# The second layer's second product with features on the partitions; joining two attention chunks' inverses in one step

## The chip, the core and the metric

One core of a Trainium2 chip runs the whole program. The metric is the device time of one execution in microseconds (us). TensorE (PE) multiplies matrices and writes to PSUM, VectorE (DVE), ScalarE (ACT) and GpSimd (POOL) work elementwise, and SyncE (SP) issues the transfers. Each engine runs its own instructions in program order and waits on semaphores for the others.

## What is computed

Attention with a state per head (the delta rule: 4 batches, 8 heads, 768 tokens, 48 dimensions), then two dense layers over its 3072 x 384 output. Cut to what matters:

```python
for t in range(S):                       # attention, k_n is k with unit norm
    y[:, :, t] = q[:, :, t] @ state
    v_old = state.T @ k_n[:, :, t]
    state += beta[t] * outer(k_n[:, :, t], v[:, :, t] - v_old)
x = y as (3072 tokens, 384)
h = x @ w_in;   x = elu(h) @ w_out       # layer 1: 384 -> 2048 -> 384
h = x @ w_in2;  out = (h * sigmoid(1.702 * h)) @ w_out2   # layer 2
```

## The kernel before

**Attention.** The sequence is cut into 12 chunks of 64 tokens, worked on in 6 passes `p` of two chunks, `a = 2p` and `b = 2p + 1`. All 32 heads of the batch are spread over the partitions, two groups of 64 tokens, and over the free axis, 16 positions `u` of a chunk. Inside a chunk the recurrence becomes a triangular system of 64 x 64 per head, and its inverse is made from halves: `gram` (L171) multiplies keys with keys, `inverse` (L194) inverts the two 32 x 32 diagonal blocks of each head on DVE, column by column, and the chunk's steps `t2`, `m1` and `m2` (L374 to L404) make the off-diagonal block, which is minus one diagonal inverse times the off-diagonal block of `gram` times the other diagonal inverse. In tile `z` columns 0 to 31 hold the diagonal inverses and columns 32 to 63 the off-diagonal blocks. `t2` transposes the chunk's inverses on DVE; `m1` is 32 products of 32 x 32 on PE into a bank `ps_b`, two copies on ACT to `m`, a third that repeats the inverses in `z`, and two clears on POOL; `m2` is 32 more products and two more moves on ACT back to `z`. Each product in fp32 stands as two MATMULs in the trace, so `m1` and `m2` are 64 records each. In passes 0 to 2 (`FINE`) the 32 x 32 blocks are themselves joined from 16 x 16 blocks by `join16` (L297; its products are L310 and L318). Then come, chunk by chunk, `kq` (keys times queries, L357) with `mask` on DVE (L368), `ks` (keys times state, L415) and the subtraction to `r` on DVE (L420), `w` (L432), `state` (L451), `y` (L467) and `out` (L489).

Nearly all of these write one PSUM tile of two banks, `ps_w` (`wide`, one buffer): the next step that takes it waits until the last one has been read.

**Dense layers.** 512 tokens (64 tokens of two chunks for 4 batches) are a block; each layer has 6 blocks, and each block 16 units `m` of 128 hidden features. A unit is `up` (9 MATMULs of 128 x 512 into `h`, L569), an activation and a split of the result into two parts `gh` and `gl` (ACT and DVE), and, two units later (`LAG`), the second product: in the first layer `down_t` (L603), 9 MATMULs with weights stationary and 512 tokens moving into three banks `acc`, features on the partitions; in the second `down_n` (L614), 12 MATMULs with `gh` or `gl` stationary and 384 output features moving into four banks out of six, tokens on the partitions. The last unit of a block copies the sums out (`end_t`, `end_n`) and stores them.

**Order.** `schedule` (L678) writes the order by hand. The first layer's blocks run with the attention of the next pass between their units: unit `u` is `fill` (DVE steps of the next `inverse`, spread by the table `VECTOR` and the function `spread`), then the list `mid` behind `up`, then the second product of unit `u - 2`, then the list `end`. A slot `2u` in the tables means `mid` of unit `u`, a slot `2u + 1` its `end`, counted from the block's first unit. The sixth block of the first layer and the second layer have no attention beside them.

Of the kernel before, what the change touches and what calls it, by code (L numbers as in the profile page):

```python
# [9 lines left out]
F32 = mybir.dt.float32  # L10
# [10 lines left out]
P = 128  # L21
# [10 lines left out]
class Kernel:  # L32
# [90 lines left out]
    def place(self, c, name):  # L123

        if c in (0, 2):
            x, i = (self.spare[0], 0) if name == "t2" else (self.spare[1], 1024)
            return x[:, i:i + 512].rearrange("p (u t) -> p u t", u=16)
        return self.ap.tile([P, 16, 32], F32, name=name, tag=name)

# [194 lines left out]


# [234 lines left out]
    def up(self, wt, x, c0, n, act_fn):  # L560
# [3 lines left out]
        c = slice(c0, c0 + n)  # L564
        hps = self.ps_m.tile([P, TB], F32, name="h", tag="h")[:, 0:n]
        i = 0
        for k in range(NK):
            for part, src in ((0, xh), (0, xl), (1, xh)):
                nc.tensor.matmul(  # L569
                    hps, wt[:, part, k * P:(k + 1) * P], src[:, k, c], start=(i == 0), stop=(i == 3 * NK - 1)  # L570
                )
                i += 1
        t = self.mp.tile([P, TB], F32, name="t", tag="t", bufs=3)[:, 0:n]
        gh = self.mp.tile([P, TB], F32R, name="gh", tag="gh", bufs=self.LAG + 1)[:, 0:n]
        gl = self.mp.tile([P, TB], F32R, name="gl", tag="gl", bufs=self.LAG + 1)[:, 0:n]
# [22 lines left out]
    def down_t(self, wt, g, acc, m):  # L598

        gh, gl = g  # L600
        for c in range(NK):
            for i, (part, src) in enumerate(((0, gh), (0, gl), (1, gh))):
                self.nc.tensor.matmul(  # L603
                    acc[c], wt[:, part, DM + c * P:DM + (c + 1) * P], src,
                    start=(m == 0 and i == 0), stop=(m == NM - 1 and i == 2),
                )

    def down_n(self, wt, g, acc, m):

        gh, gl = g  # L610
        for w in range(NW):
            c = slice(w * P, (w + 1) * P)
            for i, (src, part) in enumerate(((gh, 0), (gh, 1), (gl, 0))):
                self.nc.tensor.matmul(  # L614
                    acc[w], src[:, c], wt[:, part, DM:2 * DM],
                    start=(m == 0 and i == 0), stop=(m == NM - 1 and i == 2),
                )

    def x1_load(self, p):
# [8 lines left out]
        def split(c):  # L628

            xh, xl = [x[:, c, :].rearrange("p (b c t) -> p b c t", b=B, c=2) for x in self.x["b", p]]  # L630
            raw = st["raw"][:, c, :].rearrange("p (c b t) -> p b c t", b=B, c=2)
# [5 lines left out]
    def end_t(self, p, c0, n, acc):  # L637

        pool, tag = (self.w2p, "xo") if p >= NP - 2 else (self.mp, "w")
        d = self.x1d[p]  # L640
        halves = [pool.tile([P, 2 * DM], F32, name="xo", tag=tag, bufs=2) for _ in range(NK * n // (2 * DM))]
        if n == TB:
            x, y, n2 = *halves, n // 2
# [392 lines left out]
```

## Time and profile before

| | us |
|---|---|
| median of 3 runs | 1036.44 (1032.35 to 1042.41) |
| the profiled execution | 1037.44 |
| its span, first to last instruction | 1035.7 |
| PE busy | 982.5 (95%) |
| DVE, ACT, POOL busy | 598.6 (58%), 453.2 (44%), 49.2 (5%) |

The profile gives each engine's busy time, the chain of work that ended last (PE holds 90% of it), and the idle time of an engine before each group of instructions with what ended it. A busy time adds durations that overlap on PE, so prices of PE work are read here from one start to the next. The mean granted clock of PE was 0.981 of full speed.

### The profile page before, as it was taken

Reading aid. Unit: us, or ns where it says so; the run is one execution under the profiler, and the core shown is the slowest. Engines: PE = TensorE matmul, PEld = TensorE weight load, DVE = VectorE, ACT = ScalarE, POOL = GpSimd, SP = SyncE. Lnnn points to the kernel's source line nnn. Section 1 sums busy time; section 2 is a strip of 40 time slices with the busy share of each in tenths; the row PEclk is TensorE's granted clock in tenths of the full one; section 3 lists DMA queues with packets and bytes.
Section 4 is the critical chain, followed back from the end, with each engine's and each line's share of the span. In section 5 each row is a group of like instructions: output and inputs, shape, how many; then the busy total and the mean of one; then the engine's idle time right before and its main releaser. Section 6 shows DMA issues by size and latency. Waiting matters only on the chain.

```text
span 1035.7 us, 26881 instructions
## 1 busy us (share of the span) xinstructions
PE 982.5 (95%) x12136; PEld 837.4 (81%) x12136; DVE 598.6 (58%) x1065; ACT 453.2 (44%) x749; POOL 49.2 (5%) x65
## 2 busy tenths in 40 slices
PE   3578898999999999999999999999999999999998
PEld 3565676877788888888888788999999999999997
DVE  5579559747887788687434777643333333333333
ACT  1254465444445445445545676533333333333332
POOL 2100000000001000000000010100000001000000
PEclk9987899999999999999999999999999999999999
DMA  5252332401220221211001921001010010100000
GB/s 193 103 176 101 113 111 96 134 34 54 72 82 30 79 72 53 74 52 52 33 2 62 371 117 61 1 1 61 1 62 1 1 61 1 41 22 1 31 1 31
DMA packets 20179, 68.41 MB, mean 66 GB/s; under 512 B 3168, under 2 KB 6240, under 8 KB 20064
## 3 DMA queue, kind: packets, MB, share of 16 engines
q1 hardware_dynamic: 20064, 66.69, 18.5%
q8 instruction: 95, 1.56, 0.6%
q14 instruction: 20, 0.16, 0.1%
HBM read 57.25 MB, written 9.44 MB: 64 GB/s over the span
## 4 chain that ended last, share of the span: by engine, by line
PE 90%; DVE 5%; issue 2%; DMA 1%; ACT 1%; SPq 0%; ACTq 0%
PE h L569 39%; PE acc L603 19%; PE acc L614 10%; PE accn L614 10%; PE ps_w L467 2%; PE ps_w L357 1%; PE ps_w L183 1%; PE ps_b L399 1%; PE ps_b L384 1%; PE ps_w L415 1%; PE ps_w L432 1%; PE ps_w L451 1%; PE ps_w L489 1%; PE ps_b L310 1%; PE ps_b L318 1%
## 5 line engine op out<-in xcount | busy, mean ns | idle before, releaser
L569 PE MATMUL h<-xh,wt 128*128 128x512 f32 x1152 | 401.6, 403 | 7.3 <-DVE wt L548 5.1
L569 PEld LDWEIGHTS h<-xh,wt 128*128 128x128 f32 x1152 | 219.3, 191 | 55.0 <-DVE wt L548 7.0
L569 PE MATMUL h<-xl,wt 128*128 128x512 f32 x576 | 229.5, 398 | 0.0
L603 PE MATMUL acc<-gh,wt 128*128 128x512 f32 x576 | 198.8, 399 | 0.5 <-DVE xo L667 0.5
L591 ACT CAST gh<-t 128x512 fp32r<-128x512 f32 x192 | 119.4, 622 | 177.1 <-DVE t L582 121.0
L594 DVE TENSOR_TENSOR gl<-t,gh 128x512 fp32r<-128x512 f32 x192 | 138.4, 721 | 68.7 <-PE acc L614 31.0
L588 DVE TENSOR_TENSOR t<-t,h 128x512 f32<-128x512 f32 x96 | 66.0, 688 | 180.2 <-ACT t L585 180.1
L585 ACT ACTIVATE t<-h 128x512 f32<-128x512 f32 x96 | 57.4, 598 | 198.8 <-PE h L569 198.7
L603 PEld LDWEIGHTS acc<-gh,wt 128*128 128x128 f32 x576 | 109.7, 190 | 25.2 <-issue 1.2
L569 PEld LDWEIGHTS h<-xl,wt 128*128 128x128 f32 x576 | 110.0, 191 | 19.4 <-DVE xl L495 0.2
L603 PE MATMUL acc<-gl,wt 128*128 128x512 f32 x288 | 113.8, 395 | 0.0
L582 DVE SCALAR_TENSOR_TENSOR t<-t,h 128x512 f32<-128x512 f32 x96 | 65.7, 684 | 76.2 <-ACT t L579 75.6
L578 ACT ACTIVATE t<-h 128x512 f32<-128x512 f32 x96 | 57.4, 598 | 99.3 <-PE h L569 98.5
L614 PE MATMUL acc<-wt,gh 128*128 128x384 f32 x384 | 98.4, 337 | 0.0
L614 PE MATMUL accn<-wt,gh 128*128 128x384 f32 x384 | 98.0, 336 | 0.0
L614 PEld LDWEIGHTS accn<-wt,gh 128*128 128x128 f32 x384 | 70.9, 188 | 5.5
L614 PEld LDWEIGHTS acc<-wt,gh 128*128 128x128 f32 x384 | 70.3, 188 | 2.8
L614 PE MATMUL acc<-wt,gl 128*128 128x384 f32 x192 | 64.8, 338 | 0.0
L614 PE MATMUL accn<-wt,gl 128*128 128x384 f32 x192 | 64.7, 337 | 0.0
L603 PEld LDWEIGHTS acc<-gl,wt 128*128 128x128 f32 x288 | 55.0, 191 | 10.6
L579 ACT ACTIVATE t<-t 128x512 f32<-128x512 f32 x96 | 60.7, 632 | 3.1
L633 POOL TENSOR_TENSOR xl<-x1r,xh 128x512 fp32r<-128x512 f32 x18 | 24.1, 1339 | 412.7 <-ACT xh L632 322.1
(143 smaller groups left out, 940.0 us busy)
## 6 DMA issues: line engine op xcount, KB each, us to landing
raw<-in_w SPq DMA_DIRECT2D x32, 768.0 KB, 6.7
kt<-in_kT SPq DMA_DIRECT2D x12, 512.0 KB, 4.1
x<-in_qT SPq DMA_DIRECT2D x24, 256.0 KB, 4.1
kg<-in_kT SPq DMA_DIRECT2D x10, 512.0 KB, 4.5
vn<-in_vn SPq DMA_DIRECT2D x12, 384.0 KB, 4.0
kn<-in_kn SPq DMA_DIRECT2D x12, 384.0 KB, 3.3
x1d<-xo SPq DMA_DIRECT2D x12, 384.0 KB, 2.9
x1r<-x1d SPq DMA_DIRECT2D x6, 768.0 KB, 4.5
```

The source lines that it names most:

```text
L467: pe.matmul(ps[hf][self.tok(ab), hs(u)], g["x"][k][:, 8 * hf + u, :], su[k][:, hf, hs(u)], start=True, stop=True,)
L569: nc.tensor.matmul(hps, wt[:, part, k * P:(k + 1) * P], src[:, k, c], start=(i == 0), stop=(i == 3 * NK - 1))
L578: nc.scalar.activation(out=t, in_=hps, func=AF.Relu, scale=-1.0)
L579: nc.scalar.activation(out=t, in_=t, func=AF.Exp, scale=-1.0)
L582: nc.vector.scalar_tensor_tensor(out=t, in0=t, scalar=-1.0, in1=hps, op0=ALU.add, op1=ALU.max)
L585: nc.scalar.activation(out=t, in_=hps, func=AF.Sigmoid, scale=1.702)
L588: nc.vector.tensor_tensor(out=t, in0=t, in1=hps, op=ALU.mult)
L591: nc.scalar.copy(gh, t)
L594: nc.vector.tensor_tensor(out=gl, in0=t, in1=gh.bitcast(F32), op=ALU.subtract)
L603: self.nc.tensor.matmul(acc[c], wt[:, part, DM + c * P:DM + (c + 1) * P], src, start=(m == 0 and i == 0), stop=(m == NM - 1 and i == 2),)
L614: self.nc.tensor.matmul(acc[w], src[:, c], wt[:, part, DM:2 * DM], start=(m == 0 and i == 0), stop=(m == NM - 1 and i == 2),)
L633: nc.gpsimd.tensor_tensor(out=xl, in0=raw, in1=xh.bitcast(F32), op=ALU.subtract)
```

## The change

1. **Second layer.** `down_n` goes; both layers use one `down` with weights stationary, 512 tokens moving and three accumulators (`ps_n` banks for even blocks, `ps_m` banks for odd). The output leaves as (block, feature, token), in tiles of 512 and 256 columns, and the host brings it back to tokens by features. Tokens stay in the order of the first layer, so the split of its output into `xh` and `xl` reads straight through.
2. **Off-diagonal blocks.** For passes 1 to 5 a new `across` does `t2`, `m1` and `m2` once for both chunks. Even `u` multiply from the left first, as before; odd `u` from the right, with the transposed inverse, which puts their results in the other partitions of the same bank. `m1` so fills all 128 partitions of one bank (one copy on ACT), and `m2` writes the two banks of `ps_w` (two moves on ACT of 32 x 1024).
3. **Order.** `ks` of pass 3 to 5 moves from slot 9 to 8, `m1` from 6 to 7; other slots, and three entries of `VECTOR`, as in the diff.

```diff
-        if c in (0, 2):
+        if c == 0:
...
+    def places(self, p):
+        if p == 1:
+            t, m = self.spare[0][:, 0:1024], self.spare[1][:, 1024:1536]
+            return t.rearrange("p (u t) -> p u t", u=32), m.rearrange("p (u t) -> p u t", u=16)
+        t = self.ap.tile([P, 16, 64], F32, name="kg", tag="kg").rearrange("p u (b t) -> p (u b) t", b=2)
+        return t, self.ap.tile([P, 16, 32], F32, name="m1", tag="m1")
...
+    def across(self, p):
+        nc, pe, act = self.nc, self.nc.tensor, self.nc.scalar
+        s, own = self.pas[p], {}
+        def t2():
+            own["t2"], own["m1"] = self.places(p)
+            nc.vector.transpose(out=own["t2"], in_=s["z"][:, :, 0:32])
+        def m1():
+            z, t = s["z"], own["t2"]
+            ps = self.bank().rearrange("p (v t) -> p v t", v=16)
+            for u in range(32):
+                for o in (0, 64):
+                    near, far = slice(o, o + 32), slice(o + 32, o + 64)
+                    if u % 2:
+                        pe.matmul(ps[far, u // 2, :], z[near, u, 32:64], t[near, u, :], start=True, stop=True)
+                    else:
+                        pe.matmul(ps[near, u // 2, :], z[far, u, 32:64], z[far, u, 0:32], start=True, stop=True)
+            act.copy(own["m1"], ps)
+            act.copy(z[:, :, 32:64], z[:, :, 0:32])
+            for o in (0, 64):
+                nc.gpsimd.memset(z[o + 32:o + 64, :, 0:32], 0.0)
+        def m2():
+            z, t, m = s["z"], own["t2"], own["m1"]
+            ps = self.wide().rearrange("p b (v t) -> p b v t", v=16)
+            for u in range(32):
+                for o in (0, 64):
+                    near, far = slice(o, o + 32), slice(o + 32, o + 64)
+                    a, b = (m[far, u // 2, :], z[far, u, 32:64]) if u % 2 else (t[near, u, :], m[near, u // 2, :])
+                    pe.matmul(ps[near, u % 2, u // 2, :], a, b, start=True, stop=True)
+            for o in (0, 64):
+                near = slice(o, o + 32)
+                act.activation(
+                    out=z[near, :, 32:64].rearrange("p (v b) t -> p b v t", b=2), in_=ps[near], func=AF.Copy, scale=-1.0
+                )
...
-    def down_t(self, wt, g, acc, m):
-
+    def down(self, layer, p, m, g):
+        if m == 0:
+            self.acc = self.sums(layer, p)
         gh, gl = g
+        wt = self.wt[layer, m]
         for c in range(NK):
             for i, (part, src) in enumerate(((0, gh), (0, gl), (1, gh))):
...
-    def down_n(self, wt, g, acc, m):
...
+    def sums(self, layer, p):
+        if layer and p % 2 == 0:
+            return [self.ps_n.tile([P, TB], F32, name=f"accn{c}", tag=f"accn{c}", bufs=1) for c in range(NK)]
+        return [self.ps_m.tile([P, TB], F32, name=f"acc{c}", tag=f"acc{c}", bufs=1) for c in range(NK)]
...
+        for p in range(1, NP):
+            for name, f in zip(("t2", "m1", "m2"), self.later(lambda p=p: list(self.across(p).values()), 3)):
+                ch[2 * p][name] = f
+                del ch[2 * p + 1][name]
...
-            (4, 2, "kq"), (4, 2, "mask"), (7, 2, "nv"), (9, 2, "t2"), (9, 2, "m1"), (10, 3, "kq"), (10, 3, "mask"),
-            (11, 2, "m2"), (12, 3, "t2"), (12, 3, "m1"), (13, 2, "ks"), (14, 3, "m2"), (15, 2, "w"), (17, 2, "state"), (17, 3, "nv"),
+            (4, 2, "kq"), (4, 2, "mask"), (7, 2, "nv"), (10, 2, "t2"), (10, 3, "kq"), (10, 3, "mask"),
+            (11, 2, "m1"), (12, 2, "ks"), (13, 2, "m2"), (15, 2, "w"), (17, 2, "state"), (17, 3, "nv"),
...
-                (6, a, "t2"), (6, a, "m1"), (8, a, "m2"), (10, a, "kq"), (11, a, "ks"), (12, b, "t2"), (12, b, "m1"), (13, a, "w"), (14, b, "m2"),
+                (8, a, "kq"), (9, a, "t2"), (10, a, "m1"), (11, a, "ks"), (12, a, "m2"), (14, a, "w"),
             ) if p in self.FINE else (
-                (6, a, "t2"), (6, a, "m1"), (6, a, "kq"), (8, a, "m2"), (9, b, "t2"), (9, b, "m1"), (9, a, "ks"), (11, b, "m2"), (11, a, "w"),
+                (6, a, "t2"), (6, a, "kq"), (7, a, "m1"), (8, a, "ks"), (9, a, "m2"), (11, a, "w"),
             )
```

The order on PE in a unit of the second layer, before: the end of `up` and the second product (`accn` and `acc` are its accumulators, the bracket names what a row waits for).

```order
L569 MATMUL h<-xl,wt 128x512
L569 MATMUL h<-xh,wt 128x512
L614 MATMUL accn_8446<-wt,gh 128x384 [waits Activation_49]
L614 MATMUL accn_8446<-wt,gh 128x384
L614 MATMUL accn_8446<-wt,gl 128x384 [waits DVE_49]
L614 MATMUL accn_8447<-wt,gh 128x384 x2
L614 MATMUL accn_8447<-wt,gl 128x384
L614 MATMUL accn_8448<-wt,gh 128x384 x2
L614 MATMUL accn_8448<-wt,gl 128x384
L614 MATMUL acc_8449<-wt,gh 128x384 x2
```

And now:

```order
L616 MATMUL h<-xl,wt 128x512
L616 MATMUL h<-xh,wt 128x512
L653 MATMUL accn_9296<-gh,wt 128x512 [waits Activation_49]
L653 MATMUL accn_9296<-gl,wt 128x512 [waits DVE_49]
L653 MATMUL accn_9296<-gh,wt 128x512
L653 MATMUL accn_9297<-gh,wt 128x512
L653 MATMUL accn_9297<-gl,wt 128x512
L653 MATMUL accn_9297<-gh,wt 128x512
L653 MATMUL accn_9298<-gh,wt 128x512
L653 MATMUL accn_9298<-gl,wt 128x512
L653 MATMUL accn_9298<-gh,wt 128x512
L616 MATMUL h<-xh,wt 128x512 [waits DVE_49]
```

Twelve MATMULs of 384 columns have become nine of 512, and one weight tile's two parts now stand still instead of `gh` and `gl`.

The order on PE in the second pass, where `gram` of the third pass (L183, from `kg`) takes `ps_w`. Before, it stands behind `ks` of chunk 2 (L415):

```order
L415 MATMUL ps_w<-su_88,kt 64x48 x2
L415 MATMUL ps_w<-su_92,kt 64x48 x2
L415 MATMUL ps_w<-su_88,kt 64x48
L183 MATMUL ps_w<-kg 32x64 [waits DMAHW1_49,DVE_49]
L183 MATMUL ps_w<-kg 32x64 x63
L569 MATMUL h<-xh,wt 128x512
```

Now it stands behind the joined `m2` (L365 of the changed kernel; `gram` is L191 there, and `xl` and `xh` are spare tiles that hold `m1` and `t2`):

```order
L365 MATMUL ps_w<-xl,xh 32x32 x2
L365 MATMUL ps_w<-z,xl 32x32 x2
L191 MATMUL ps_w<-kg 32x64 [waits DMAHW1_49,PE_49,Activation_49]
L191 MATMUL ps_w<-kg 32x64 x63
L616 MATMUL h<-xh,wt 128x512
L616 MATMUL h<-xl,wt 128x512
```

`gram` waited for DVE, which reads `ks` out of `ps_w`; now it waits for ACT, which reads `m2` out of it.

The order on DVE in the fifth pass around `r`, behind the first `t2`, the mask and the first steps of the next pass's `inverse`; before (L594 is `gl` of unit 3, L582 the activation of unit 4, L375 `t2` of chunk b, L420 the subtraction to `r`, the others steps of `inverse`):

```order
L240 SCALAR_TENSOR_TENSOR na<-na,dg 128x32
L241 SCALAR_TENSOR_TENSOR nb<-nb,na 128x32
L594 TENSOR_TENSOR gl<-t,gh 128x512
L582 SCALAR_TENSOR_TENSOR t<-t,h 128x512
L375 STREAM_TRANSPOSE t_4805<-z 128x512
L420 TENSOR_TENSOR r<-vn,ps_w 128x768
L239 RECIPROCAL na<-nb 128x32
```

And now (L641 is `gl`, L468 the subtraction to `r`, L629 the activation):

```order
L248 SCALAR_TENSOR_TENSOR na<-na,dg 128x32
L249 SCALAR_TENSOR_TENSOR nb<-nb,na 128x32
L641 TENSOR_TENSOR gl<-t,gh 128x512
L468 TENSOR_TENSOR r<-vn,ps_w 128x768
L629 SCALAR_TENSOR_TENSOR t<-t,h 128x512
L247 RECIPROCAL na<-nb 128x32
L248 SCALAR_TENSOR_TENSOR na<-na,dg 128x32
```

The second transposition is gone from here (the first, ahead of the mask, now has 128 x 1024), and `r` stands ahead of unit 4's activation.

## Rows read from the trace of the kernel before

**Rows 1.** Busy time by stage: stretch, length, each engine's busy time (instructions), granted clock, DMA.
```profile
300.00:571.00 271.00, 270.47 (x4067) 220.93 (x4066) 182.66 (x361) 134.82 (x221) 8.77 (x14) 1.00 0.16 52
...
627.00:1027.74 400.74, 400.74 (x2008) 362.59 (x2007) 161.13 (x227) 141.19 (x235) 19.41 (x15) 1.00 0.06 22
```

**Rows 2.** Chain that ended last, second layer: start us, us, what.
```profile
642.90 2.08 PE h L569 x9
...
1018.12 1.58 PE acc L614 x9
1019.70 2.08 PE h L569 x9
```

**Rows 3.** Timeline of PE, first layer without attention: start us, us, engine, line, operation.
```profile
581.36 0.39 PE L569 MATMUL h<-xh,wt 128*128 128x512 f32 x1
...
583.40 0.39 PE L603 MATMUL acc<-gh,wt 128*128 128x512 f32 x1
...
622.16 0.39 PE L569 MATMUL h<-xh,wt 128*128 128x512 f32 x1
```

**Rows 4.** Timeline of PE, attention's third pass (idle time before and its releaser in brackets).
```profile
211.79 1.26 PE L310 MATMUL ps_b<-kg,z 32*32 32x16 f32 x128
...
215.25 1.38 PE L318 MATMUL ps_b<-w 16*32 16x16 f32 x128
...
237.75 1.15 PE L415 MATMUL ps_w<-su,kt 48*64 48x48 f32 x64 [0.74 <-DVE x L368]
...
244.48 1.15 PE L432 MATMUL ps_w<-r,z 64*64 64x48 f32 x64
...
247.83 1.20 PE L399 MATMUL ps_b<-m,t 32*32 32x32 f32 x64
...
251.22 0.94 PE L451 MATMUL ps_w<-su,kn 64*48 64x48 f32 x64
```

**Rows 5.** Timeline of PE, attention blocks of the fourth and fifth pass.
```profile
349.04 1.15 PE L415 MATMUL ps_w<-su,kt 48*64 48x48 f32 x64
...
354.43 1.15 PE L432 MATMUL ps_w<-r,z 64*64 64x48 f32 x64
...
375.14 2.07 PE L467 MATMUL ps_w<-su,x 128*64 128x48 f32 x64
...
403.80 1.20 PE L384 MATMUL ps_b<-z 32*32 32x32 f32 x64
...
410.37 1.20 PE L399 MATMUL ps_b<-m,t 32*32 32x32 f32 x64
...
413.76 1.20 PE L384 MATMUL ps_b<-z 32*32 32x32 f32 x64
...
420.28 1.20 PE L399 MATMUL ps_b<-m,t 32*32 32x32 f32 x64
...
426.79 0.94 PE L451 MATMUL ps_w<-su,kn 64*48 64x48 f32 x64
```

**Rows 6.** Timeline of DVE beside the first of those blocks, fifth pass.
```profile
405.14 0.72 DVE L375 STREAM_TRANSPOSE t<-z 128x512 f32<-128x512 f32 x1
406.16 2.80 DVE L368 TENSOR_TENSOR x<-ps_w,mask_p 64x512 f32<-64x512 f32 x4 [0.30 <-PE ps_w L357]
...
412.79 0.68 DVE L582 SCALAR_TENSOR_TENSOR t<-t,h 128x512 f32<-128x512 f32 x1
413.38 0.70 DVE L375 STREAM_TRANSPOSE t<-z 128x512 f32<-128x512 f32 x1
416.11 0.96 DVE L420 TENSOR_TENSOR r<-vn,ps_w 128x768 f32<-128x768 f32 x1 [2.02 <-PE ps_w L415]
```

**Rows 7.** Timeline of PE, then of ACT: the product of `gram` behind `ks`, second pass.
```profile
139.73 1.47 PE L183 MATMUL ps_w<-kg 48*32 48x64 f32 x127 [1.08 <-DVE r L420]
...
141.25 1.01 ACT L189 COPY z<-ps_w 128x1024 f32<-128x1024 f32 x1 [2.83 <-PE ps_w L183]
```

**Rows 8.** Busy time and granted clock in two stretches of the second pass.
```profile
123.40:133.70 10.30, 9.82 (x89) 7.63 (x90) 6.97 (x10) 2.77 (x5) 0.00 (x0) 0.50 0.07 17
```

## Prediction before the run

> **What bounds the kernel now.** First the busy time by stage: from 300 us on PE is busy all the time (270.47 of 271.00 us beside the last passes of attention, 400.74 of 400.74 in the second layer) at a granted clock of 1.00, while DVE has 182.66 and 161.13 [rows 1]. So past 300 us time is the sum of what PE does, and every microsecond that PE saves is a microsecond of the kernel, unless a saving makes PE wait. The reader should then leave busy times aside, since records on PE overlap, and measure from start to start. Two such clocks tick in the trace. In the second layer a unit's `up` starts at 642.90 and, 90 units later, at 1019.70 [rows 2]: 376.80 / 90 = 4.187 us for 9 MATMULs of 512 columns and 12 of 384. In the first layer, where no attention is left, `up` starts at 581.36 and ten units later at 622.16 [rows 3]: 4.080 us for 18 MATMULs of 512 columns, and `up` alone takes 583.40 - 581.36 = 2.04.
>
> Attention's blocks stand between these products. With 2.04 for half a unit, a block's price is the distance to the next block less 2.04 for each half between. In the third pass `m2` of one chunk (64 records) costs 251.22 - 247.83 - 2.04 = 1.35, `w` 247.83 - 244.48 - 2.04 = 1.31, and the 128 records of `join16` 215.25 - 211.79 - 2.04 = 1.42 [rows 4]. That 128 small products cost hardly more than 64 is the point on which the second part rests.
>
> **Second layer.** Both layouts stream the same columns (12 x 384 = 9 x 512 = 4608), so nothing is gained by columns. But the changed unit has exactly the shapes of the first layer's unit, stationary weights of 128 x 128 and 512 columns moving, and that one's time is in the trace. I take it: 4.187 - 4.080 = 0.107 less for each of 94 units, and for the last two second products, which have no `up` beside them, (4.187 - 2.08) - 2.04 = 0.067 each: 94 x 0.107 + 2 x 0.067 = **10.2 us**. The trace does not show these shapes with the second layer's activation beside them; it shows them with the first layer's, which has DVE and ACT busier, and PE did not wait there. The evacuations and stores keep their number and bytes and lie beside PE; at the very end four moves and four stores remain as before, which I cost at nothing (half a microsecond either way).
>
> The Trainium skill has a rule that speaks against this gain: "TensorE: Matmul & The Clock Gate", section "Back-to-back issue gap", gives a MATMUL of N columns N/2.4 + 2.5 ns. By it, as an estimate, 12 steps of 384 take 1950 ns and 9 of 512 take 1942 ns, and the layer would gain 0.7 us, not 10.2. The measured steps do not follow it: 2.04 us for nine is 227 ns each [rows 3], and 4.187 - 2.08 for twelve is 176 ns each [rows 2].
>
> **Off-diagonal blocks, PE.** The number of small products stays: `m1` and `m2` of two chunks, 64 records each, become two blocks of 128. What changes is that a block now goes round four places of the array (rows and columns of 32) where it went round two. No row shows these blocks. From below they are bounded by the fastest row of 128 records, `join16`'s L310, 1.26 us, which also goes round four places [rows 4]. From above by twice the present record, 2 x 1.20, plus the 0.15 that a block costs beyond its records (1.35 - 1.20): 2.55. I take 1.42, by the row of the same tile height and the same four places. One objection is that in `m2` even and odd `u` share columns of the array. Two rows answer it: `y` (L467), whose two places share all rows and not the columns, takes 2.07 us, and `ks` (L415), with as many records and the same weight width, whose four places share columns pairwise, takes 1.15 [rows 5]. Sharing columns did not cost it.
>
> Passes 3, 4 and 5. Before: `m1` with `kq` 410.37 - 403.80 - 4.08 = 2.49; `m2` 413.76 - 410.37 - 2.04 = 1.35; `m1` with `ks` 420.28 - 413.76 - 4.08 = 2.44; `m2` with `w` 426.79 - 420.28 - 4.08 = 2.43; together 8.71 [rows 5]. Now five blocks stand alone: `kq`, `ks` and `w` at 1.31 (`ks` alone: 354.43 - 349.04 - 4.08 [rows 5]; `w` above; `kq` taken as `ks`), `m1` and `m2` at 1.42: 6.77. Saved 1.94 a pass.
>
> What this makes late: `m2` now writes `ps_w`, so it waits until DVE has read `ks` out of it, and behind `m2` on PE stands everything. In the fifth pass DVE was free for `r` at 416.11 - 2.02 = 414.09. The second transposition (0.71) and unit 4's activation (0.59) no longer stand ahead, and the first transposition is twice as long (0.72 more, of which DVE's idle 0.30 takes a part): 414.09 - 0.71 - 0.59 + 0.42 = 413.21, and `r` takes 0.96 [rows 6], so `ps_w` is free at 414.17. PE would be there at 403.80 + 1.31 + 2.04 + 1.42 + 2.04 + 1.31 + 2.04 = 413.96. So a new wait of 0.2 to 0.3; I take 0.3, for passes 3 and 4. In pass 5 no `inverse` is beside it and nothing waits. If the transposition of 128 x 1024 took half as much again (0.7 more), the waits would be 0.7 longer each. Sum: 2 x (1.94 - 0.3) + 1.94 = **5.2 us**.
>
> Pass 2. Before, four blocks at 1.35; now two at 1.42: 2.56 saved. `kq` moves a unit ahead, so the 0.74 that `ks` waited for the mask [rows 4] should go. Against that, `m1` now needs `t2` (odd `u`): 1.44 of transposition, plus 1 us that I allow for the join's last subtraction and copy ahead of it, less the `up` of 2.04 in between: 0.35, between 0 and 1. 2.56 + 0.74 - 0.35 = **2.95 us**.
>
> Pass 1. Again 2.56. But `gram` of the third pass stands right behind `m2`, in the same `ps_w`. It waited 1.08 us for DVE's `r`; now it waits for two moves of 32 x 1024 on ACT, and a move of 1024 columns takes 1.01 [rows 7]: at least 2.0, and up to 3 if ACT comes to them late. I take 2.5, 1.4 more than before: **1.15 us**. The cover that hides ACT's moves elsewhere, two products between `m2` and `w`, is missing only here.
>
> ACT and POOL have fewer and longer instructions (three copies and two moves for ten), which frees ACT; I cost it at nothing, since past 300 us no engine but PE sets the end.
>
> **Sum.** 10.2 + 5.2 + 2.95 + 1.15 = 19.5 us off the profiled execution's 1037.44: 1017.9. The median of the runs is 1.0 below the profiled execution, so the prediction is **1017 us**.
>
> **The rivals.**
> - *The blocks do not overlap.* If four places go no faster than two, a block costs 2.55, not 1.42. For `m2` alone that is 5 x 1.13 = 5.7 and 1023; for both 11.3 and 1028. For it: no row has these places. Against it: L310 and L415 as above.
> - *The 384-column step is not what costs.* If the second layer's 0.107 came from what lies beside PE there and not from the shape, the new unit would take 4.187 again: 1017 + 10.2 = 1027. Against it: between 642.90 and 1019.70 most units have one activation beside them and DVE has 161.13 us in 400.74 [rows 1, 2], against a denser first layer that is faster. By the rule of the Trainium skill named above ("TensorE: Matmul & The Clock Gate"), the layer's gain would be 0.7 and the time some 1026.5.
> - *The clock falls.* In the second pass, from 123.40 to 133.70, the granted clock was 0.50, that is 1.2 GHz instead of 2.4, while DVE and ACT were mostly idle [rows 8]. It fell in a stretch of small products with waits between, and the change lies just there, with a longer wait of `gram`. One more such stretch costs 10.3 x 0.5 = 5.2: 1022; two, 1027. One fewer gives 1012.
> - *The other side: each turn drains the array.* If alternating between two directions made every small product run alone, as in `y`, where 64 records take 2.07 [rows 5], a block would take 4.14 + 0.15 = 4.3, 2.9 more, and ten blocks 29 us: 1046, slower than before. It decides from 1.42 + 19.5 / 10 = 3.4 us a block. Against it: L310 and L415 change place with every product. "TensorEngine Tiling (Array Packing)", section "Key Properties", of the Trainium skill says that a change of tiling mode drains TensorE; the blocks keep one tile size, and no run here shows a mode change by itself.
>
> **How the numbers follow.** The sum as it stands 0.62 (its own range 1012 to 1022); no overlap 0.12 (`m2` alone 0.07, both 0.05); the step 0.05; the clock worse 0.15; the drain 0.03; better than the sum by a clock stretch fewer and no new waits 0.03. A measurement of this kernel can tell about 1%: faster is below 1026, slower above 1047. Faster: 0.62 + 0.07 + 0.12 (of the clock) + 0.03 + 0.01 = 0.85. Same: 0.05 + 0.04 + 0.03 + 0.01 = 0.13. Slower: 0.02 of the drain. The range 1009 to 1027 takes in the sum, the better case, `m2` alone, and nearly all of the clock: some 0.86, with the drain and both blocks left out.
>
> **What would show it.** Second layer: `up` to `up` 4.08 us to the end. Blocks: `m1` and `m2` with 128 records in about 1.25 us, one each a pass; 2.4 would be the first rival, 4 the last. Waits: `m2` for DVE's `r` in passes 3 and 4 by some tenths, `gram` behind `m2` for ACT by 2 to 3 us near 135 us, none in pass 5. Clock: 0.50 in no more stretches than before. The prediction is wrong if the second layer keeps 4.19, if a block is over 2 us, or if PE waits more than 3 us in all past 200 us.

## The result and the profile after

The changed kernel took 1020.54 us (median of 4 runs, 1015.85 to 1026.91) beside 1035.67 us of the kernel before (median of 4 runs on the same chip): a ratio of 0.985, 95% interval 0.981 to 0.989. That is 15 us of a predicted 19.5, inside the range of 1009 to 1027. Three further series of the same two kernels, below, gave 0.986, 0.981 and 0.984. The runs of the changed kernel lie further apart than those of the kernel before (20 runs: 1013.8 to 1029.4, standard deviation 4.3; 50 runs: 1031.3 to 1042.6, 2.6), and most of this study is about why.

The profiled execution was one of the short ones, 1015.85 us, 21.6 less than the profiled one of before. Busy time by stage, as in [rows 1] (stretch, length, each engine's busy time and instructions, granted clock, DMA share, GB/s):

```profile
300.00:558.00 258.00, 257.55 (x3915) 209.09 (x3914) 176.39 (x344) 124.07 (x198) 8.21 (x8) 1.00 0.17 53
611.00:1005.00 394.00, 394.00 (x1740) 326.25 (x1739) 163.99 (x231) 143.21 (x238) 19.78 (x15) 1.00 0.07 23
```

PE is as full as it was, at a granted clock of 1.00, so whatever it saved past 300 us is in the time. The second layer in the chain that ended last (start us, us, what), as in [rows 2]:

```profile
985.76 2.04 PE h L616 x9
...
1002.08 2.04 PE h L616 x9
```

Four units from `up` to `up` take 16.32 us, 4.08 each, where [rows 2] had 4.187: the first layer's pace to the hundredth. The same chain in the last pass of attention, where [rows 4, 5] had four blocks for the pair of chunks:

```profile
486.57 1.08 PE ps_w L463 x64
487.65 2.27 PE acc L653 x9
489.92 1.22 PE ps_w L365 x82
491.13 2.26 PE h L616 x9
493.40 2.04 PE acc L653 x9
495.44 1.08 PE ps_w L480 x64
```

L463 is `ks`, L365 the new `m2` (of its 128 records the chain counts 82, since they overlap), L480 `w`. From `ks` to `w` are 8.87 us with three half units of 2.04 between: 2.75 for `ks` and `m2` together. `m2` takes 1.22 for its 128 records, the 1.2 that 64 took before [rows 5].

In the second pass (pass 1, as passes are counted from 0), `gram` behind `m2` (timeline of PE, idle time before and its releaser in brackets), and the DVE rows in the fifth pass on which a term rested, `t2` (L341), the mask (L416) and `r` (L468):

```profile
134.82 2.19 PE L191 MATMUL ps_w<-kg 48*32 48x64 f32 x128 [2.14 <-ACT z L368]
```

```profile
396.65 1.24 DVE L341 STREAM_TRANSPOSE kg<-z 128x1024 f32<-128x1024 f32 x1
397.82 2.76 DVE L416 TENSOR_TENSOR x<-ps_w,mask_p 64x512 f32<-64x512 f32 x4
...
403.56 0.95 DVE L468 TENSOR_TENSOR r<-vn,ps_w 128x768 f32<-128x768 f32 x1
```

`gram` waited for ACT's two moves, 2.14 us, as foreseen (2.5). `r` did not come late: it began at 403.56, 0.06 after `ks` had ended, and was through 1.2 us before `m2` began at 405.69. So the new wait of `m2` that I had put at 0.3 in two passes isn't there.

### The profile page after: what moved, and what is told of

The parts are those of the page before. It is cut to its first block, busy times and chain, and to the rows that moved or that the text cites. A ratio compares the mean times of both kernels' runs of the same rounds, so it can differ in the third digit from the quotient of the medians.

```text
span 1014.1 us, 26233 instructions
## 1 busy us (share of the span) xinstructions
PE 961.2 (95%) x11848; PEld 787.4 (78%) x11848; DVE 598.5 (59%) x1060; ACT 441.0 (43%) x719; POOL 48.6 (5%) x55
## 4 chain that ended last, share of the span: by engine, by line
PE 91%; DVE 4%; issue 2%; DMA 2%; ACT 1%; SPq 0%; ACTq 0%; DVEq 0%
PE h L616 39%; PE acc L653 29%; PE accn L653 10%; PE ps_w L515 2%; PE ps_w L191 1%; PE ps_w L405 1%; PE ps_w L463 1%; PE ps_w L480 1%; PE ps_w L499 1%; PE ps_w L537 1%; PE ps_b L326 1%; PE ps_b L318 1%; DMA raw<-in_w 1%; DMA kg<-in_kT 1%; DVE wt L596 1%
## 5 line engine op out<-in xcount | busy, mean ns | idle before, releaser
L653 PE MATMUL acc<-gh,wt 128*128 128x512 f32 x864 | 293.4, 394 | 0.5 <-DVE xo L714 0.5
L653 PEld LDWEIGHTS acc<-gh,wt 128*128 128x128 f32 x864 | 163.1, 189 | 35.8 <-issue 0.9
L641 DVE TENSOR_TENSOR gl<-t,gh 128x512 fp32r<-128x512 f32 x192 | 138.7, 722 | 70.6 <-ACT gh L638 70.4
L653 PE MATMUL acc<-gl,wt 128*128 128x512 f32 x432 | 169.1, 391 | 0.0
L629 DVE SCALAR_TENSOR_TENSOR t<-t,h 128x512 f32<-128x512 f32 x96 | 65.7, 684 | 75.5 <-ACT t L626 74.9
L653 PE MATMUL accn<-gh,wt 128*128 128x512 f32 x288 | 96.4, 389 | 0.0
L653 PEld LDWEIGHTS acc<-gl,wt 128*128 128x128 f32 x432 | 81.7, 189 | 16.5 <-DVE gl L641 0.3
L653 PEld LDWEIGHTS accn<-gh,wt 128*128 128x128 f32 x288 | 54.1, 188 | 11.2
L653 PE MATMUL accn<-gl,wt 128*128 128x512 f32 x144 | 56.0, 389 | 0.0
L585 DVE SCALAR_TENSOR_TENSOR w<-raw,w 128x768 uint32<-128x768 uint32 x32 | 33.7, 1053 | 0.9
L416 DVE TENSOR_TENSOR x<-ps_w,mask_p 64x512 f32<-64x512 f32 x44 | 30.2, 685 | 5.6 <-PE ps_w L405 5.1
L191 PE MATMUL ps_w<-kg 48*32 48x64 f32 x1280 | 17.2, 251 | 16.6 <-DMA kg<-in_kT 12.6
```

Source lines behind the costliest of these rows:

```text
L191: self.nc.tensor.matmul(o[q:q + 32], k[:, 32 * sub:32 * sub + 32], x, start=True, stop=True)
L416: v.tensor_tensor(out=g["x"][k][self.tok(k), 8 * hf:8 * hf + 8], in0=i, in1=self.mask_p[t].unsqueeze(1).to_broadcast(list(i.shape)), op=AL ...
L585: v.scalar_tensor_tensor(out=bits[m], in0=words(m, 0), scalar=29, in1=bits[m], op0=ALU.logical_shift_right, op1=ALU.bitwise_or)
L629: nc.vector.scalar_tensor_tensor(out=t, in0=t, scalar=-1.0, in1=hps, op0=ALU.add, op1=ALU.max)
L641: nc.vector.tensor_tensor(out=gl, in0=t, in1=gh.bitcast(F32), op=ALU.subtract)
L653: self.nc.tensor.matmul(self.acc[c], wt[:, part, DM + c * P:DM + (c + 1) * P], src, start=(m == 0 and i == 0), stop=(m == NM - 1 and i == 2),)
```

## The experiments

Each profiled execution can be cut at two points that all kernels have: the first `state` of pass 1 (chunk 2) and that of pass 5 (chunk 10, the last pass), both rows of 64 products on PE. The kernel before and the changed one, in the timelines of PE:

```profile
152.19 0.94 PE L451 MATMUL ps_w<-su,kn 64*48 64x48 f32 x64
...
512.66 0.94 PE L451 MATMUL ps_w<-su,kn 64*48 64x48 f32 x64
```

```profile
148.64 0.94 PE L499 MATMUL ps_w<-su,kn 64*48 64x48 f32 x64
...
500.75 0.94 PE L499 MATMUL ps_w<-su,kn 64*48 64x48 f32 x64
```

The table has all profiles of this study cut so, in us. "Stands" counts the places in passes 2 to 5 where PE stopped for over a microsecond inside `m2`.

| kernel | execution | to `state` of pass 1 | passes 2 to 5 | rest of the span | stands in `m2` |
|---|---|---|---|---|---|
| before | 1037.44 | 152.2 | 360.5 | 523.1 | 0 |
| l2_only | 1029.39 | 153.8 | 360.6 | 513.3 | 0 |
| across_only | 1036.60 | 154.3 | 357.6 | 523.0 | 1 |
| changed | 1015.85 | 148.6 | 352.1 | 513.4 | 0 |
| after_third | 1016.55 | 150.0 | 351.4 | 513.4 | 0 |
| after_fourth | 1025.02 | 148.8 | 361.2 | 513.3 | 2 |
| after_again | 1029.39 | 153.1 | 361.2 | 513.3 | 2 |
| two_places | 1022.60 | 149.4 | 358.2 | 513.3 | 0 |
| v_late | 1021.80 | 149.4 | 357.3 | 513.4 | 1 |
| v_late_gram | 1017.95 | 147.2 | 355.7 | 513.4 | 1 |
| m2_split | 1020.92 | 152.2 | 353.6 | 513.4 | 0 |
| m2_split3 | 1021.61 | 152.8 | 353.6 | 513.5 | 0 |
| halves2 | 1033.49 | 152.0 | 353.1 | 526.7 | 0 |

**The two halves of the change, each alone.** One kernel has the diff's second layer only (`up`, `down`, `sums`, `end_x1`, `end_out` and the layout of `out`), the other its blocks only (`places`, `across`, the slots, `VECTOR`).

> Only the second layer's change: down products of 512 columns with the weights held still; the off-diagonal blocks as in the kernel before. My sum gives 10.2 us off the kernel before (a unit of layer 2 goes from 4.19 to 4.08 us, the stretch before layer 2 stays where it was). The rival that the 384-column step is not what costs gives at most 0.7 us. If the change gained by something that needs both halves, this one and across_only together give clearly less or more than the whole.

> Only the off-diagonal blocks of both chunks at once, with their new places in the order; layer 2 as before. My sum gives 9.3 us off the kernel before (passes 3 to 5: 5.2, pass 2: 2.95, pass 1: 1.15); the trace of the changed kernel read stage by stage says 12 (passes 3 to 5: 5.1, pass 2: 4.0, pass 1: 4.0, less 0.8 for a stretch of half clock). Layer 2 keeps 4.19 us a unit.

Beside 1037.29 us of before, l2_only took 1028.57 (4 runs; ratio 0.991, 0.987 to 0.995) and across_only 1032.94 (10 runs: nine between 1022.24 and 1037.08, and one of 1043.42 that the ratio leaves out; 0.995, 0.992 to 0.999). The second layer's gain is in the right place and has the right size: the table's last part is 9.8 us shorter in l2_only and 0.1 in across_only. The blocks alone gave 4.4 us in the median where 9.3 were expected, with a spread of 15 us among the nine. The waits of PE past 200 us in the profile of across_only (what, released by, total us, times, longest) begin with a line that the kernel before does not have (its longest "issue" there is 0.8, in `join16`):

```profile
PE ps_w L365 <- issue: 2.7, 1, 2.7
```

**The changed kernel again.** Nothing edited; the second of these series stands beside the v load's experiment, the third beside the split.

> The changed kernel unaltered, to see how far its own runs lie apart: its first four were 1015.85, 1016.23, 1024.86 and 1026.91 us. If the 10 us between the pairs belong to the chip or to the run, the new ones fall at about 1016 and at about 1025 again, and the profile of a long one has the ten microseconds in one place (a load at the start, a fetch, a stretch of half clock). If they were an accident of that one session, all lie within 3 us of each other.

> The changed kernel unaltered once more, as the measure for the others of this call: 1016 to 1029 us by its eight runs so far, about 1020 in the middle. In its long profile (1029.39 us) the second product of the blocks stood 2.8 us with nothing to wait for in the third and the sixth pass, while a 16 KB block of PE's instructions came in only behind the packets of a v load; in its short profile (1015.85 us) it did not. If that is what parts long runs from short ones, a profile of this run shows such stands when it is long and none when it is short.

> The changed kernel unaltered, as the measure for the split beside it: 1014 to 1029 us by its fourteen runs so far (mean 1020.5). Its profile has a stand of 2 to 3 us in a second product if a 16 KB block of PE's instructions begins to come in over a microsecond late there, and none if it does not.

1020.83 us (4 runs), 1018.06 (6) and 1021.01 (6), beside 1037.29, 1039.73 and 1036.45 of before. Two of the profiles fell on long executions and one more on a short one, and the table parts them: with no stand passes 2 to 5 take 351.4 and 352.1, with two 361.2. Nine microseconds lie there, and the whole gain of the blocks with them, since before had 360.5. The last pass of after_fourth, to be read against the chain of the changed kernel above:

```profile
494.75 1.12 PE ps_w L365 x76
495.86 2.54 issue
498.40 0.31 PE ps_w L365 x11
498.71 3.13 PE h L616 x9
501.84 2.80 PE acc L653 x9
504.64 1.08 PE ps_w L480 x64
```

PE stops for 2.54 us near the end of `m2` and waits for nothing that the profile shows ("issue"). The two half units behind it take 3.13 and 2.80 instead of 2.26 and 2.04. Busy time and granted clock of the stand, and of the stretch behind it:

```profile
495.86:498.40 2.54, 0.00 (x1) 0.00 (x0) 0.00 (x0) 0.00 (x0) 0.00 (x0) 1.00 0.03 8
499.90:503.30 3.40, 3.40 (x9) 2.64 (x8) 0.13 (x1) 2.12 (x3) 0.00 (x0) 0.50 0.02 5
```

After the stand the granted clock was 0.50 (1.2 GHz of 2.4) for 3.40 us, though PE had work without a gap. So this stand cost 2.5 us and some 1.7 more behind it (half of 3.40). Of the seven stands that the table counts, five are followed by such a stretch. The other stand of after_fourth has 2.62 and 1.7 more, which makes 8.6 of the nine microseconds.

What PE lacks there are instructions, as the rest of this section shows. `m2` is 128 MATMULs and as many weight loads, 256 instructions in 1.3 us; elsewhere a whole unit of 4.08 us has 36. PE's instructions come in by DMA queue q8 in blocks of 16 KB: 93 blocks for the 23788 instructions of the changed kernel, 99 for the 25520 of halves2, so some 256 to a block. Traffic by queue (packets, MB, share) from the start of `ks` to the start of `m2`, first in the short execution of the changed kernel, then in after_fourth, and last in after_fourth from the start of `m2` to the end of the stand:

```profile
q1 hardware_dynamic: 16, 0.05, 8.8%
q8 instruction: 1, 0.02, 2.4%
```

```profile
q1 hardware_dynamic: 20, 0.06, 7.5%
```

```profile
q1 hardware_dynamic: 124, 0.33, 25.2%
q8 instruction: 1, 0.02, 1.6%
```

In the short execution the block comes in before `m2` begins (at 488.00, `m2` at 489.85), in after_fourth while `m2` runs (496.08, `m2` at 494.68). That holds for every profile in which `m2` is whole: without a stand in passes 2 and 5 the block began at least 1.2 us ahead of `m2`, with one it began between 0.2 us ahead of it and 1.6 behind.

The count of instructions says the same. Number PE's instructions in order of time from the start of the trace (weight loads, MATMULs and PE's own waits): the seven stands come after 10177 of them (pass 2) or 18369 (pass 5), both 193 more than a multiple of 256. In the thirteen profiles of the table PE stands 124 times for over half a microsecond before 560 us without a semaphore to wait for. Every one of the 124 comes after such a number of instructions, and each time PE goes on 1.2 to 1.6 us after a block has come in. So the stands are borders between blocks of instructions. They are not new: the kernel before has eight of them before its first `state` of pass 1, 12.7 us in all, and one in `join16`, beside the row that the prediction took for its price:

```profile
224.07 0.46 PE L310 MATMUL ps_b<-kg,z 32*32 32x16 f32 x34 [0.83 <-issue]
```

What the change did is to put `m2` there. At these two borders the 256 instructions up to the border lasted 6.5 and 6.2 us in the kernel before; in the short execution of the changed kernel they last 3.4.

The Trainium skill ("Runtime: NRT & Kernel Launch", section "Instruction fetch mechanics") has an engine's instructions refilled in blocks of 16 KiB, 256 instructions, and calls a block's border mostly hidden. The blocks agree; hidden it is at these places in the kernel before, and not in the changed one when a block comes late.

**Is it the load in front of the block?** In both long profiles the v load of the second chunk (q1 above, 384 KB) came in just then. In v_late it is held back until ACT is through with `m2`'s copies; v_late_gram moves chunk 5's `gram` away from behind `m2` too.

```diff
+        if gate:
+            self.nc.scalar.copy(t[:, 0, 0:1], self.one)
...
-        at(end, 7, lambda: self.load_v(3))
+        at(end, 7, lambda: self.load_v(3, gate=True))
...
-            at(end, o + 5, lambda b=b: self.load_v(b))
+            at(end, o + (6 if late else 5), lambda b=b: self.load_v(b, gate=True))
...
-                self.passes(at, spread, end, fill, p, (3, 6), (9, o + 2), lambda: turned(2))
+                self.passes(at, spread, end, fill, p, (3, 5), (9, o + 2), lambda: turned(2))   # v_late_gram only
```

> The changed kernel with the v load of the second chunk of passes 1 to 5 held back until ScalarE is through with the copies of the second product (a one-column copy into its tile ahead of it, and in pass 2 one unit later), so that it no longer runs while that product's 256 instructions are fetched. Theory (the load in front of the fetch is what stalls the product): no stand of 2 to 3 us in the second product, all runs between 1013 and 1021, median about 1016, some 4 us under the changed kernel's of this call. Rival (the runs part by the half-clock stretches alone, 37 to 44 us of them per run): the median and the spread stay as they are, within 1 us and 3 us.

> The same with the Gram product of chunk 5 half a unit earlier, beside the first product of pass 1 and not behind the second, where it waits 2.14 us for ScalarE's copies. If that wait is what I missed of pass 1's gain, the product waits under 0.5 us there and the state of chunk 2 comes 1.5 to 2.1 us earlier than in v_late; total about 1014. If the clock or another engine sets the end of that stretch, the wait goes and the state comes less than 0.7 us earlier.

v_late took 1021.25 us (6 runs, 1015.23 to 1027.55), no less than the changed kernel beside it (1018.06), and its last pass has a stand of 1.71 us. In that stretch no data moved at all. Chain, then traffic from 492 to 498 us:

```profile
492.35 1.12 PE ps_w L367 x76
493.47 1.71 issue
495.17 0.31 PE ps_w L367 x11
495.48 3.78 PE h L618 x9
```

```profile
q8 instruction: 1, 0.02, 1.4%
```

The block came late (492.22, `m2` at 492.28) with its road empty, so a block can be late without the load, and the load as the one cause fell. It may still make a late block later. In the five stands with the load beside, the block began 1.4 to 1.6 us behind the start of `m2`, among the load's last packets, and PE stood 2.54 to 2.83 us; in the two without, of v_late and v_late_gram, it began 0.1 and 0.2 us ahead, and PE stood 1.71 and 1.38. v_late_gram (1018.77, 5 runs, 1017.95 to 1022.89, where 1014 were expected) lost the wait of 2.14 for ACT and got another in its place: `gram` now stands right behind `m1`, 512 instructions in a row, and the chain of the second pass shows 1.47 us of "issue" before its second half, and 1.22 inside `m2`. Its `state` of pass 1 came 2.2 us earlier than in v_late, about what was expected if the wait for ACT was what that pass lacked, but less than the same stretch varies between executions of one kernel.

```profile
126.75 1.47 issue
128.22 1.04 PE ps_w L193 x61
...
134.91 0.92 PE ps_w L367 x64
135.83 1.22 issue
```

**What the four places bring.** The same products, even heads first, then odd ones, in both blocks:

```diff
-            for u in range(32):
+            for u in (*range(0, 32, 2), *range(1, 32, 2)):
```

> The changed kernel with the same products of the blocks in another order: all even heads first, then all odd ones, so that two places of the array take turns at a time and not four. My theory (four places in turn are what makes a block of 128 records cost 1.3 us) expects a block of 2.4 us, ten blocks so, 1.1 us each: 9 to 11 us more than the changed kernel, and passes 3 to 5 longer by 2.2 each. The rival (the saving came from making one block of two, with fewer copies and changes between blocks, and not from the places) expects blocks of 1.3 us and no change beyond 1 us.

1022.51 us (4 runs, 1022.02 to 1024.03). The last pass:

```profile
492.54 1.08 PE ps_w L463 x64
...
495.89 2.05 PE ps_w L365 x126
...
502.24 1.08 PE ps_w L480 x64
```

`m2` takes 2.05 us with two places in turn and 1.22 with four; from `ks` to `w` 9.70 for 8.87. So a block costs 0.83 more, and passes 2 to 5, with eight blocks, take 6 to 7 us more than in the executions of the changed kernel without stands. The places are the cause, at a smaller price than the 1.1 a block that I had named. No stand fell in `m2` here, but the profile cannot say whether a slower block rides out a late block of instructions, since none was late: in passes 2 and 5 they began 1.8 and 1.7 us ahead of `m2`. Four runs within 2 us of each other hint at it, but they are four.

**Cutting `m2`.** Half of it, 128 instructions, at its slot and half one slot later, in passes 2 to 5; the copies behind the second half (m2_split) or behind each half (m2_split2). m2_split3 is m2_split2 with `m2` of pass 1 cut too, and chunk 5's `gram` behind `w`.

```diff
-                (8, a, "kq"), (9, a, "t2"), (10, a, "m1"), (11, a, "ks"), (12, a, "m2"), (14, a, "w"),
+                (8, a, "kq"), (9, a, "t2"), (10, a, "m1"), (11, a, "ks"), (12, a, "m2"), (13, a, "m2b"), (14, a, "w"),
...
-                (6, a, "t2"), (6, a, "kq"), (7, a, "m1"), (8, a, "ks"), (9, a, "m2"), (11, a, "w"),
+                (6, a, "t2"), (6, a, "kq"), (7, a, "m1"), (8, a, "ks"), (9, a, "m2"), (10, a, "m2b"), (11, a, "w"),
```

> The changed kernel with the second product of passes 2 to 5 cut in two halves of 64 products, half a unit apart, with the copies behind the second half. A half takes 128 instructions at once and not 256. Theory (a block of 256 instructions that comes late by 2 to 3 us stands the array only where the whole next block is eaten in 1.3 us): no stand in the second product in any pass, the passes 2 to 5 as in the changed kernel without stands (96, 84.5, 87.5, 84.3 us from state to state), all runs under 1021, median 2 to 4 us below the changed kernel's. Rival (stands fall where they will, or the half-clock stretches alone part the runs): median within 1 us of the changed kernel's and runs up to 1027 still. If w, one slot behind the second half, has to wait for the copies, 0.5 us or more show there in each pass.

> The split of the second product in passes 2 to 5 again, now with ScalarE's copies behind each half, so that only half of them stand between the second half and w. In the split's profile w waited 0.4 us for them in passes 3, 4 and 5. If that is so, these waits go (1.3 us in all), no second product of passes 2 to 5 stands, and the runs lie between 1015 and 1021, median about 1018. If the stands in second products were chance and not tied to 256 instructions at once, some run goes above 1024 as in every series of the changed kernel so far, and the profile of it has a stand there.

> The same, with the second product of pass 1 cut too and the Gram product of chunk 5 one unit later, behind w, instead of right behind the second product. There it waited 2.1 us for ScalarE in nearly every profile, and stood 1 to 2.5 us more in four of six with nothing to wait for. If these are what kept pass 1 from its gain, the stretch from the first up product to the state of chunk 2 falls from 69.7 to 76.7 us (changed kernel, four profiles) to 68 to 73, and the total to 1014 to 1017. If the half-clock stretches there set its length, it stays in 70 to 77 and the total with m2_split2.

1018.91 us for m2_split (5 runs, 1017.19 to 1022.10), beside 1021.01 of the changed kernel; 1019.91 for m2_split3 (6 runs, 1014.95 to 1023.07); five runs of m2_split2 lie between 1019.92 and 1027.26, and its profiled execution, at 5247.93, gives no rows. Runs over 1024 were the sign that I had named for stands by chance, and two of the five are clearly over it; no profile tells what they stood for. Passes 2 to 5 took 353.6 in the two profiles, with no stand over a microsecond inside a half. The price of m2_split is the wait that I had named, `w` for the copies, 0.4 us in three passes (the chain calls it "issue", but ACT's second copy ends just then, at 500.37):

```profile
494.19 0.68 PE ps_w L367 x50
...
497.13 0.68 PE ps_w L367 x50
...
500.08 0.38 issue
500.47 1.15 PE ps_w L484 x64
```

In passes 2 and 5 of the two profiles the block began in time, 1.7 us ahead of `m2`, at all places but one, and these say nothing of the cut. The one late block is in pass 2 of m2_split3: it began at 241.38, 1.5 us behind the start of `m2` (239.89). There the second half reads:

```profile
242.91 0.48 PE ps_w L367 x38
243.40 0.20 issue
243.59 0.39 PE ps_w L367 x24
```

From its first product to its last, `m2` took 4.09 us there for 3.71 elsewhere, so a block as late as those behind the stands of 2.5 to 2.8 us cost 0.4.

But the 16 runs of the three together have a mean of 1020.9, the 20 of the changed kernel 1020.5. So no better kernel came of it. In m2_split3 pass 1 from the first `up` to `state` took 70.5 us, inside what was expected, but the first `up` itself came at 82.3 instead of 75.5, and nothing was left of it.

**What a product costs beside its columns.**

```diff
+                for n in (slice(0, 256), slice(256, 512)) if layer else (slice(0, 512),):
...
-                    self.acc[c], wt[:, part, DM + c * P:DM + (c + 1) * P], src,
...
+                        self.acc[c][:, n], wt[:, part, DM + c * P:DM + (c + 1) * P], src[:, n],
```

> The changed kernel with each down product of layer 2 cut into two of 256 columns, with the same weights each time: 18 products a unit for 9. By the rows of before and after, a product costs its columns over 2.4 GHz and some 14 ns more (384 columns 176 ns, 512 columns 227 ns): 18 x (106.7 + 14) = 2.17 us a unit for 2.04, 12 us more in all. With 2.5 ns a product (the other reading of the same saving) it is 0.02 us a unit and 2 us in all. If a weight load of 128 columns does not fit under 256 columns of product, more than 12.

1033.49 us in one run, 13 more than the changed kernel's mean; the last part of the table grew by 13.3, where 12 were expected. The chain:

```profile
802.06 2.15 PE accn L655 x18
804.22 2.07 PE h L616 x9
806.28 2.15 PE accn L655 x18
```

A unit takes 4.22 for 4.08, 0.14 more for nine more products and not one column more: some 15 ns a product. The steps are now 227 ns for 512 columns, 176 for 384 and 2.15 / 18 = 119 for 256: each the columns at 2.4 GHz and some 13 to 16 ns more. The 2.5 ns of "TensorE: Matmul & The Clock Gate" (section "Back-to-back issue gap" of the Trainium skill) do not hold for these products with a weight load each; that section itself gives them for a product alone, and says that in a stream of weight loads and products both set the spacing. Not all of the gain is in these steps. Of the 0.107 a unit, 0.067 lies in the second product (4.187 - 2.08 = 2.107 before, 2.04 now) and 0.04 in `up`, which took 2.08 beside products of 384 columns, takes 2.07 beside those of 256 and 2.04 beside its own shape; no run isolates why.

## Why the prediction was right, and where it was not

- **Second layer, 10.2 us: right.** The rest of the span past pass 5 is 9.6 to 9.8 us shorter in every kernel that has it (the end of the kernel after PE's last product, which I had costed at nothing, takes 0.4 more: PE's part alone is 10.1), 4.08 us a unit, and halves2 shows that a product costs some 15 ns beside its columns. That is the cause of 0.067 of the 0.107 a unit; the 0.04 in `up` came in with the row of the whole unit, and its cause stays open. The rival that the 384-column step does not cost anything fell.
- **Blocks, 1.42 each: right.** From `m1` to the next block and from `m2` to `w` are 1.44 beyond the half units, in passes 3 and 5; two_places shows 2.27 without the rotation. The rival "blocks do not overlap" fell, and that each turn drains the array, too.
- **Passes 3 to 5, 5.2 us: right in the sum, with two errors in it.** In the changed kernel's profile they save 1.68, 1.69 and 1.72. I had 1.94, less 0.3 for `r` in two of them. The wait for `r` does not exist; against it `m1` and `m2` cost 1.44 and not 1.42, and `m1` 0.25 more in pass 4, a stand that ends at 399.9, at a border of instruction blocks (after 15553 instructions, again 193 more than a multiple of 256). Some 0.2 in passes 3 and 5 is left without a cause.
- **Pass 2, 2.95 us:** 3.3 in the same profile (99.0 to 95.8 us from `state` to `state`). By its own terms `m1`'s wait for `t2` is 1.44 + 1 - 2.04 = 0.40, not 0.35; that changes nothing here.
- **Pass 1, 1.15 us: borne out only as an estimate.** `gram`'s wait was 2.14 for a foreseen 2.5. But the stretch up to `state` varies from 148.6 to 154.3 in six profiles with the changed order, mean 151.1, and had 152.2 and 153.8 in the two with the old. The 3.6 us that the first pair of profiles shows must not be read as the change's gain; 1.9 is the difference of the means, with a spread larger than itself. Stands of over half a microsecond at instruction borders go with it. In the six they come to 9.0, 11.7, 12.4, 13.7, 14.6 and 14.9 us up to `state`, for 148.6, 148.8, 150.0, 152.0, 153.1 and 154.3; in the two to 12.7 for 152.2 and 14.2 for 153.8. A straight line through the six puts the changed order 1.0 and 1.2 us ahead at these sums: an estimate from eight profiles, and near 1.15. Stretches at half clock, 24 to 38 us of them, vary too, and no run parts the two.
- **Luck.** The first pair of profiles comes out 21.6 us apart for a sum of 19.5, but 3.7 us of that are fewer stands before the first `state` of pass 1 (9.0 for 12.7), and no stand fell in `m2`.
- **What failed: the sum has no term for instructions that come late.** By my own test the prediction is wrong "if PE waits more than 3 us in all past 200 us"; in the first profile it doesn't, in after_again and after_fourth it does, by `m2` alone (2.62 and 2.54 us in after_fourth). I had weighed semaphores, engines and the clock, and not the supply of instructions. Merging two blocks of 64 products into one of 128 that runs twice as fast made a stretch of 256 instructions in 1.3 us, and there a block of instructions that comes late stops PE. Two of four profiles of the changed kernel have two such stands, and half-clock stretches with them: 9 us, the whole gain of passes 2 to 5. The medians of four series gained 15 to 22 us and the mean of all runs 17 (1037.5 to 1020.5), which is less than the sum; only the profiled runs tell how many stands each had. The rival of the clock came true in part: half-clock stretches past 200 us, 1.7 us each, but behind stands of PE for instructions. In the first profile, though, one such stretch begins in `gram`'s wait:

```profile
134.40:141.20 6.80, 6.38 (x138) 5.34 (x139) 0.00 (x0) 2.28 (x5) 0.00 (x0) 0.50 0.20 47
```

In return the stretch of before from 123.40 on [rows 8] is gone, so the sum up to the first `state` of pass 1 is 30.7 us at half clock for 34.1. [rows 8] had been read as a stretch with DVE mostly idle; DVE was busy there for 6.97 of 10.30 us.

What stays open: why a block of PE's instructions sometimes begins 1.5 to 3.5 us late. The v load is not needed for it, as v_late shows, though the latest blocks all had the load beside them; and the program is the same in short and long executions. Whether cutting `m2` shortens the runs is likewise open: the one late block that met a cut `m2` says so, the runs do not. The stretch before the first `state` of pass 1 alone moves the time by 5 us, and no experiment here was about it.

## What to carry to other kernels

A product of 384 columns costs about as much beside its columns as one of 512, so lay a long chain out so that it has the fewest products, and price it by the same shape elsewhere in the trace. Small products that go round four places of the array went 1.7 times as fast here as round two, but count the instructions: a stretch of 256 in little over a microsecond uses up a whole block, and PE stands if the next one is not in. Look for "issue" among PE's waits before the change, too: it was there. And where a kernel's runs spread, profile a long one and a short one and cut both at the same points before a difference between two kernels is read from one profile of each.

## What the runs showed of the hardware

- PE stood 1.4 to 2.8 us inside the 128 small products of `m2`, waiting for nothing that the profile shows, at 7 places in 5 profiles; each time a 16 KB block on the instruction queue began between 0.2 us ahead of the products and 1.6 us behind their start, and in v_late with no other traffic beside it.
- All 124 stands of PE over half a microsecond that no semaphore explains (13 profiles, up to 560 us) fall where the count of PE's instructions is 193 more than a multiple of 256, and end 1.2 to 1.6 us after a 16 KB block has come in.
- The stand of 2.54 us in after_fourth was followed by 3.40 us at a granted clock of 0.50 while PE was busy throughout. The profiles of before and the two short ones of the changed kernel have no such stretch between 200 us and the last product.
- 128 products of 32 x 32 and 32 columns: 1.22 us with four places in turn, 2.05 with two.
- Behind its columns a product of 128 x 128 weights costs 13 to 16 ns (119, 176 and 227 ns for 256, 384 and 512 columns).
